# The last two groups' output projection as one stripe of 16 rows in three pieces

## The chip, the cores and the metric

The kernel runs on one core of one Trainium2 chip. The metric is the device time of one execution in microseconds (us); lower is better. A run's time is a little longer than the span that its profile shows, which goes from the first to the last instruction.

## The reference

Two independent problems, A and B, of the same shape: one decoding step of attention over a sliding window, followed by the output projection. Batch 2, one query token, D = 576, 32 query heads over 16 key/value heads of 128, cache length 16384, of which the last W = 4096 keys count; bf16.

```python
q = (x @ wq).reshape(B, Sq, Hq, Dh)            # heads first
k = repeat(k_cache[:, :, Sk - W:, :], 2)       # the last 4096 keys
v = repeat(v_cache[:, :, Sk - W:, :], 2)
p = softmax((q @ k.T) * Dh ** -0.5)
out = (p @ v).reshape(B, Sq, Hq * Dh) @ wo     # wo is 4096 x 576
...
return concatenate([a, b], axis=-1)            # 2 x 1 x 1152
```

## The kernel before

The work is cut into groups of four key/value heads: 4 groups per problem, 8 in all (NG = 8; groups 0 to 3 are A, 4 to 7 are B). A group has one K slab and one V slab per batch, 4 MB each, so 16 K slabs and 16 V slabs (NSLAB = 16). Slab i belongs to group i // 2 and batch i % 2. The slabs pass through `ring`, a buffer of four slots.

All large transfers are issued by SyncE (SP) in one order, the list `stream`: K slabs, V slabs three steps behind (LAG = 3), and now and then a piece of wo. `issue` writes one entry with the operations that it waits for, and `ensure` issues entries up to the one needed. SP waits in order: what stands behind a waiting transfer waits too.

Per group: VectorE (DVE) turns K (`make_X`), TensorE (PE) makes scores (`make_S`), the maximum goes over PE, DVE and GpSimd (POOL) (`make_max`, `make_Tm_pe`, `make_nM`, `make_bias`), ScalarE (ACT) takes exponentials, DVE turns them (`make_pT`), and PE multiplies with V (`make_PV`, 128 matmuls of 512 columns for a slab, four at a time into the bank `OTB`). `make_evac` scales the result into `tmp` and sums it into `oR`. `make_dg` spreads `oR` over partitions with one matmul into the bank TB, by a 0/1 matrix, and `make_pick` takes from that the value that each partition needs: a product with a mask on DVE (A) and a reduction. Then PE multiplies with rows of wo held in `wob` (16 rows of 576 columns on each of 128 partitions).

The projection of groups 0 to 5 goes by pairs: two groups are one stripe of wo, 16 rows in one transfer of 2304 KB ("M"), the first group on partitions 0 to 63 of `oM` and the second on 64 to 127 (`make_projm`). The last two groups, 6 and 7, are handled one by one: each has 8 rows ("W", 1152 KB), all 128 partitions belong to the one group, and the picked values lie in `oP`, spread by the matrix `selx` and picked by the mask `cm16` (`make_proj`). Group 6's 8 rows are one transfer; group 7's are three, cut by

```python
w_cuts = [0, 4, 7, 8]
```

The last row's weights are loaded ahead of its data, and its four matmuls come in two operations, one for each half of the columns that DVE and ACT evict at the end (`make_E`). For problem B each row is four matmuls of 144 columns (`cells`: two column halves at two places of the array). The last V slab arrives in two pieces, cut at key 80 of 128. `filler` puts matmuls on PE whose result nobody reads.

The end of the program is written out by hand. After the last K slab, in the order in which PE gets it: V slab 13, rows 0 to 7 of stripe 2 (groups 4 and 5), the spreading of group 6, rows 8 to 11, the sums of group 7, V slab 14, rows 12 to 15, fillers, V slab 15's first piece, spreading and pick of group 7's batch 0, fillers, V slab 15's second piece, fillers, spreading and pick of batch 1, the W rows of group 6, the W rows of group 7, the evictions and the output.

Of the kernel before, what the change touches and what calls it, by code (L numbers as in the profile page):

```python
# [63 lines left out]
def build_kernel(nc, probs, out):  # L64
# [29 lines left out]
    with es:  # L94
# [21 lines left out]
        cm16 = sb("cm16", [128, 16], FP32)  # L116
        jmask_f = sb("jmask_f", [128, 8], FP32)
        m8 = sb("m8", [128, 16, 8], FP32)
        selx = sb("selx", [128, 8, 16], FP32)
# [13 lines left out]
        oP = sb("oP", [128, 2, 8, Bb], BF16)  # L133
        oM = sb("oM", [128, 16, Bb], BF16)
# [25 lines left out]
        v_cuts = [0, 80, KJ]  # L160
        lastv_sem = [sem("lastv")]
        w_cuts = [0, 4, 7, 8]
# [54 lines left out]
        def mask(dst, view, axes, tag):  # L217
            return dve(lambda e: e.tensor_reduce(dst, view, axes, ALU.add), [p_ident_f], tag)
# [21 lines left out]
        d_cm = mask(cm16[:, 0:16], ident_f[:].rearrange("p (x q) -> p q x", q=16), AX.X, "cm16")  # L240
# [6 lines left out]
        p_sx = pool(lambda e: e.tensor_copy(selx[:], jmask_f[:, 0:8].unsqueeze(2).broadcast_to([128, 8, 16])), [d_jf], "selx")  # L247
# [83 lines left out]
        stream.append(("W", NG - 2))  # L331
        stream.append(("W", NG - 1))
        NM = NG // 2 - 1
# [13 lines left out]
        projm_first = {}  # L347

        def issue(key):
            kind, i = key  # L350
            if kind in "MW":
                n = 16 if kind == "M" else 8
                first_g = 2 * i if kind == "M" else i
                P, gl = first_g // GP, first_g % GP
                at = 0 if kind == "M" else 8 * (i % 2)
                rows = probs[P][4][gl * 1024:gl * 1024 + 128 * n, :].rearrange("(p j) n -> p j n", j=n)
                deps = ([projm_op[i - 1]] if i >= 1 else []) if kind == "M" else [projm_first[NM - 1] if i == NG - 2 else projm_op[NM - 1]]
                cuts = [(0, n, wo_sem[i % 2])]
                if i == NG - 1:
                    cuts = [(w_cuts[k], w_cuts[k + 1], ([wo_sem[1]] + lastw_sem)[k]) for k in range(3)]  # L360
                stream_dma[key] = []
                for j0, j1, sm in cuts:
                    def f(e, j0=j0, j1=j1, sm=sm):
                        return e.dma_start(wob[:, at + j0:at + j1, :].rearrange("p j n -> p (j n)"),
                                           rows[:, j0:j1, :].rearrange("p j n -> p (j n)")).then_inc(sm, 16)
                    stream_dma[key].append((j0, j1, dma_op("sp", sm, 1, f, deps, "wo%d_%d" % (i, j0))))
                return
            P, g, b = i // (2 * GP), (i // 2) % GP, i % 2
            src_t = probs[P][1] if kind == "K" else probs[P][2]
            src = src_t[b, 4 * g:4 * g + 4, Sk - W:Sk, :].rearrange("k (r j) d -> r k j d", j=KJ)  # L370
            r = slot_of[key]
            prior = uses[r][:uses[r].index(key)]
            deps = [last_reader[prior[-1]]] if prior else first_deps[r]
            cuts = [(0, KJ, ring_sem[r])]
            if key == ("V", NSLAB - 1):
                cuts = [(v_cuts[k], v_cuts[k + 1], ([ring_sem[r]] + lastv_sem)[k]) for k in range(2)]
            stream_dma[key] = []
            for c0, c1, sm in cuts:
                def f(e, c0=c0, c1=c1, sm=sm):
                    return e.dma_start(ring[:, r, c0 * 128:c1 * 128],  # L380
                                       src[:, :, c0:c1, :].rearrange("r k j d -> r k (j d)")).then_inc(sm, 16)
                stream_dma[key].append((c0, c1, dma_op("sp", sm, 1, f, deps, "%s%d_%d" % (kind, i, c0))))
# [23 lines left out]
        proj_op = {}  # L406
# [166 lines left out]
        def make_dg(G, bs=(0, 1)):  # L573
            b0, nb = bs[0], len(bs)
            sl_, p_sl = (selx, p_sx) if G >= NG - 2 else (selm, p_sm)
            n, bank, op = tb_job(lambda e, bank: e.matmul(bank[:, 0:128 * nb], sl_[:].rearrange("p h c -> p (h c)"),
                                                          oR[:, b0:b0 + nb, :].rearrange("p b d -> p (b d)"), start=True, stop=True),
                                 "dg%d_%d" % (G, b0), [ch[(G, "red%d" % b)] for b in bs] + [p_sl])
            ch[(G, "dg")] = op
            dg_job[(G, bs)] = (n, bank)  # L580

        def make_pick(G, bs=(0, 1)):
# [3 lines left out]
            tv = tmp[:, 0:128 * nb]  # L586
            if G < NG - 2:
                h0 = 64 * v
                tv = tmp[h0:h0 + 64, 0:256]
                a = dve(lambda e: e.tensor_tensor(  # L590
                    tv.rearrange("p (b c j) -> p b c j", b=2, c=8), bank[h0:h0 + 64, 0:256].rearrange("p (b c j) -> p b c j", b=2, c=8),
                    jmask_f[h0:h0 + 64, 0:8].unsqueeze(1).unsqueeze(3).broadcast_to([64, 2, 8, 16]), ALU.mult),
                    [ch[(G, "dg")], d_jf, ch["tmp"]], "A%d" % G)
                dst, q = oM[h0:h0 + 64, :, :].rearrange("p j b -> p b j"), G // 2
                free, c = [projm_op[q - 1]] if q >= 1 else [], 8
            else:
                a = dve(lambda e: e.tensor_tensor(
                    tv.rearrange("p (b c j) -> p b c j", b=nb, c=16), bank[:, 0:128 * nb].rearrange("p (b c j) -> p b c j", b=nb, c=16),
                    cm16[:, 0:16].unsqueeze(1).unsqueeze(3).broadcast_to([128, nb, 16, 8]), ALU.mult), [ch[(G, "dg")], d_cm, ch["tmp"]], "A%d" % G)
                dst = oP[:, v, :, b0:b0 + nb].rearrange("p j b -> p b j")  # L600
                free, c = [], 16
            tb_consumer[n] = a

            def f_pick(e):
                with nc.allow_low_precision(reason="one term of the c is not zero"):
                    return e.tensor_reduce(dst, tv.rearrange("p (b c j) -> p b j c", b=nb, c=c), AX.X, ALU.add)
# [14 lines left out]

        def make_projm(q, j0=0, j1=16):
            P, start = 2 * q // GP, (2 * q) % GP == 0 and j0 == 0
            ensure(("M", q))
# [13 lines left out]
            deps = [ch[(2 * q, "oP", 0)], ch[(2 * q + 1, "oP", 0)], stream_dma[("M", q)][0][2]]  # L638
            if start:
                deps += [e_ops[(P - 1, 0)], e_ops[(P - 1, 1)]] if P >= 1 else [q_ev[2]]  # L640
            projm_op[q] = pe(f, deps, "projm%d_%d" % (q, j0))
            if j0 == 0:
                projm_first[q] = projm_op[q]

        def make_proj(G):
            v = G % 2
            ensure(("W", G))
            oPs = [ch[(G, "oP", b)] for b in range(2) if (G, "oP", b) in ch]
            for j0, j1, dma in stream_dma[("W", G)]:
                held = G == NG - 1 and j1 == 8  # L650
                if held:
                    def f_w(e):
                        for h in range(2):
                            last = e.add_instruction(mybir.InstLdweights(
                                name=nc.get_next_instruction_name(), engine=mybir.EngineType.PE,
                                ins=[e.lower_ap(oP[:, v, 7, :], for_matmul_weights=True)], outs=[],
                                tile_size=(128, 32), tile_position=(0, 32 * h)))
                        return last
                    pe(f_w, oPs, "projw%d" % G)

                    for c in range(2):
                        def f_c(e, c=c):
                            for h in range(2):
                                last = cell(e, oP[:, v, 7, :], 8 * v + 7, c, h, False, True)
                            return last
                        last_cell[c] = pe(f_c, oPs + [dma], "proj%d_7%d" % (G, c))
                    continue

                def f(e, j0=j0, j1=j1):
                    for j in range(j0, j1):  # L670
                        last = cells(e, oP[:, v, j, :], 8 * v + j, False)
                    return last
                proj_op[G] = pe(f, oPs + [dma], "proj%d_%d" % (G, j0))

        def make_E(P):
# [7 lines left out]
            for h in range(2):  # L683
                def f_first(e, h=h):
                    return e.dma_start(out[:, 0, h * NH:(h + 1) * NH], out_sb[:, h * NH:(h + 1) * NH]).then_inc(out_sem, 16)
                dma_op(("sp", "act")[h], out_sem, 1, f_first, [e_ops[(0, 0)], e_ops[(0, 1)], stream_dma[("W", NG - 1)][1][2]], "out0_%d" % h)
# [61 lines left out]
        make_projm(NM - 1, 0, 8)  # L748
        make_dg(NG - 2)
        make_projm(NM - 1, 8, 12)  # L750
# [5 lines left out]
        make_projm(NM - 1, 12, 16)  # L756
        filler(4)
        make_evac(i + 2)
        make_PV(i + 3, (0,))
        make_dg(NG - 1, (0,))  # L760
        make_pick(NG - 1, (0,))
        filler(4)
        make_PV(i + 3, (1,))
# [4 lines left out]
        make_proj(NG - 2)  # L768
        make_proj(NG - 1)
# [93 lines left out]
```

## Time and profile before

| | before |
|---|---|
| median of 3 runs | 363.09 us (362.92 to 363.18) |
| profiled execution | 363.1 us |
| its span | 361.8 us |
| mean granted TensorE clock | 0.887 |
| busy PE / DVE / ACT / POOL | 63% / 60% / 13% / 7% |
| traffic | 153.28 MB, mean 424 GB/s |
| wo of B, last two groups: issue to landing | 1152 KB 19.4 us; 576 KB 10.2; 432 KB 10.9; 144 KB 10.8 |

How to read it: the span is what the profile covers; 1.3 us of the profiled execution lie outside. A busy share is an average over the whole span, and an engine can be idle for most of it and still set the end. A transfer's time to landing holds its time in the queue: all transfers share 16 DMA engines, which work through them in the order of issue, each on its part of every transfer. In a timeline row the columns are the start, the duration, engine, line, operation, output and inputs, count, and in brackets the idle time before it with what ended that. A line of a view by windows has, for each engine, the busy time and the number of instructions, then the granted clock (1.00 is full speed), the share of the DMA engines and GB/s.

### The profile page before, as it was taken

Reading aid. Unit: us, or ns where it says so; the run is one execution under the profiler, and the core shown is the slowest. Engines: PE = TensorE matmul, PEld = TensorE weight load, DVE = VectorE, ACT = ScalarE, POOL = GpSimd, SP = SyncE. Lnnn points to the kernel's source line nnn. Section 1 sums busy time; section 2 is a strip of 40 time slices with the busy share of each in tenths; the row PEclk is TensorE's granted clock in tenths of the full one; section 3 lists DMA queues with packets and bytes.
Section 4 is the critical chain, followed back from the end, with each engine's and each line's share of the span. In section 5 each row is a group of like instructions: output and inputs, shape, how many; then the busy total and the mean of one; then the engine's idle time right before and its main releaser. Section 6 shows DMA issues by size and latency. Waiting matters only on the chain.

```text
span 361.8 us, 2701 instructions
## 1 busy us (share of the span) xinstructions
PE 229.0 (63%) x1357; PEld 56.1 (16%) x943; DVE 218.6 (60%) x150; ACT 45.4 (13%) x77; POOL 24.3 (7%) x84
## 2 busy tenths in 40 slices
PE   0397687767464866671696656662776675667575
PEld 0010111112110211120121211110112121112222
DVE  0811898495949392924919493952927776675522
ACT  1002100040031002200005000500005000500500
POOL 4200101100010001000010000000010000001000
PEclk9999698969999889888798998899589897869989
DMA  8999999999999999999999999999999999999996
GB/s 327 449 428 420 442 426 424 446 413 446 417 447 420 442 422 422 439 438 420 438 424 434 431 438 412 448 420 442 424 435 429 428 438 420 434 442 420 427 417 258
DMA packets 6088, 153.28 MB, mean 424 GB/s; under 512 B 684, under 2 KB 828, under 8 KB 1084
## 3 DMA queue, kind: packets, MB, share of 16 engines
q1 hardware_dynamic: 6056, 153.10, 98.7%
q8 instruction: 9, 0.15, 0.2%
q14 instruction: 3, 0.02, 0.0%
q10 hardware_dynamic: 20, 0.01, 0.0%
HBM read 153.10 MB, written 0.00 MB: 423 GB/s over the span
## 4 chain that ended last, share of the span: by engine, by line
DMA 49%; DVE 24%; PE 16%; issue 8%; ACT 1%; POOL 1%; SPq 0%
DMA ring<-in_B_k_cache_dram 25%; DVE xt L436 15%; DMA ring<-in_B_v_cache_dram 9%; DMA ring<-in_B_wq_dram 7%; DMA ring<-in_A_k_cache_dram 6%; PE st L266 6%; PE st L462 5%; DMA wob<-in_B_wo_dram 3%; DVE oR L569 2%; DVE mx L470 2%; DVE pT L509 2%; PE pj L266 2%; DVE tmp L562 2%; PE ot L539 1%; ACT pR L500 1%
## 5 line engine op out<-in xcount | busy, mean ns | idle before, releaser
L462 PE MATMUL st<-xt,zq 128*128 128x512 bf16 x256 | 119.3, 466 | 93.6 <-DVE xt L436 93.6
L436 DVE STREAM_TRANSPOSE xt<-ring 128x4096 f32<-128x4096 f32 x32 | 141.6, 4429 | 33.5 <-DMA ring<-in_A_k_cache_dram 18.2
L266 PE MATMUL st<-xt,zq 128*128 128x512 bf16 x256 | 118.0, 461 | 0.0
L500 ACT ACTIVATE pR<-st,bias 128x512 bf16<-128x512 f32 x32 | 40.0, 1419 | 219.0 <-DVE bias L493 219.0
L462 PEld LDWEIGHTS st<-xt,zq 128*128 128x128 bf16 x256 | 28.3, 110 | 211.5 <-DVE xt L436 110.0
L539 PE MATMUL ot<-ring,pT 128*32 128x512 bf16 x512 | 32.0, 393 | 8.3 <-DMA ring<-in_B_v_cache_dram 8.3
L493 DVE SCALAR_TENSOR_TENSOR bias<-vmask,tb,offm 128x4 f32<-128x4 f32 x8 | 1.8, 224 | 37.1 <-PE tb L490 37.1
L523 DVE TENSOR_REDUCE ssum<-tb 128x2 f32<-128x8 f32 x8 | 1.3, 162 | 33.4 <-PE tb L520 33.4
L428 POOL TENSOR_TENSOR zq<-qs,bmask 128x64 bf16<-128x64 bf16 x32 | 8.6, 292 | 161.2 <-PE st L266 140.3
L509 DVE STREAM_TRANSPOSE pT<-pR 128x2048 bf16<-128x2048 bf16 x8 | 18.4, 2303 | 0.7 <-ACT pR L500 0.7
L562 DVE SCALAR_TENSOR_TENSOR tmp<-ot,rsb,dmask 128x512 f32<-128x512 f32 x16 | 11.5, 719 | 9.4 <-PE ot L539 9.4
L281 PE MATMUL ot<-ring,pT 128*32 128x512 bf16 x18 | 7.6, 421 | 15.1 <-DMA ring<-in_A_wq_dram 14.5
L539 PEld LDWEIGHTS ot<-ring,pT 128*32 128x32 bf16 x512 | 12.4, 99 | 23.7 <-DMA ring<-in_B_v_cache_dram 10.5
L569 DVE TENSOR_REDUCE oR<-tmp 128x128 f32<-128x512 f32 x15 | 15.6, 1039 | 0.5
L266 PE MATMUL pj<-ring,pT 128*32 128x512 bf16 x36 | 12.1, 422 | 0.0
L266 PE MATMUL pj<-wob,oM 128*2 128x288 bf16 (+1 forms) x64 | 10.2, 256 | 0.0
L470 DVE TENSOR_REDUCE mx<-st 128x2 f32<-128x1024 f32 x8 | 9.7, 1208 | 0.1
L500 ACT ACTIVATION_READ_ACCUMULATOR pR<-st,bias 128x1 f32 x32 | 9.1, 283 | 0.0
L636 PE MATMUL pj<-wob,oM 128*2 128x288 bf16 x32 | 7.9, 286 | 0.0
L224 DVE TENSOR_TENSOR xt<-xt,hmask 4x1152 bf16<-4x1152 bf16 x2 | 2.8, 1398 | 8.4 <-DMA xt<-in_A_x_dram 8.4
L266 PE MATMUL st<-ring,pT 128*32 128x512 bf16 x18 | 7.4, 414 | 0.0
L472 POOL TENSOR_TENSOR mv<-mx,v 128x2 f32<-128x2 f32 x8 | 1.6, 195 | 80.0 <-DVE mx L470 80.0
(71 smaller groups left out, 79.5 us busy)
## 6 DMA issues: line engine op xcount, KB each, us to landing
ring<-in_A_k_cache_dram SPq DMA_DIRECT2D x8, 4096.0 KB, 24.9
ring<-in_A_v_cache_dram SPq DMA_DIRECT2D x8, 4096.0 KB, 30.0
ring<-in_B_k_cache_dram SPq DMA_DIRECT2D x8, 4096.0 KB, 28.5
ring<-in_B_v_cache_dram SPq DMA_DIRECT2D x7, 4096.0 KB, 31.8
ring<-in_A_wq_dram SPq DMA_DIRECT2D x1, 4608.0 KB, 13.6
ring<-in_B_wq_dram SPq DMA_DIRECT2D x1, 4608.0 KB, 24.1
wob<-in_A_wo_dram SPq DMA_DIRECT2D x2, 2304.0 KB, 29.8
ring<-in_B_v_cache_dram SPq DMA_DIRECT2D x1, 2560.0 KB, 26.9
```

What stands on the lines that cost most here:

```text
L266: return e.add_instruction(mybir.InstMatmult(name=nc.get_next_instruction_name(), engine=mybir.EngineType.PE, ins=[e.lower_ap(mv_), e.lowe ...
L281: last = e.matmul(QB[c], wt, mv_, start=first, stop=True, skip_group_check=True)
L428: last = e.tensor_tensor(dst, src, msk, ALU.mult)
L436: Xop[(t, jh)] = dve(lambda e: e.transpose(xt[:, jh, :].bitcast(FP32).rearrange("p (kp x kt) -> p x kp kt", kp=2, kt=2), ring[:, r, jh * H ...
L462: last = e.matmul(ob, wt, mv_, start=first, stop=True, skip_group_check=True)
L470: ch[(G, "max")] = dve(lambda e: e.tensor_reduce(mx[:], st[:, :].rearrange("p (x t) -> p t x", t=2), AX.X, ALU.max), [Sop[(2 * G + 1, 1)]] ...
L500: last = e.activation(pR[:].rearrange("p (x k) -> p k x", k=4)[:, kv, :], st[:, :].rearrange("p (x t) -> p t x", t=2)[:, kv % 2, :], ACTF.Exp,
L509: pT_op[G] = dve(lambda e: e.transpose(pT[:, v, :].rearrange("p (w j q) -> p j w q", w=4, q=8), pR[:].rearrange("p (j w q) -> p j w q", w= ...
L539: last = e.matmul(OTB[32 * c:32 * c + 32, :], pT[:, v, base + 32 * c:base + 32 * c + 32], ring[:, r, jj * 128:(jj + 4) * 128], start=rd == ...
L562: evac_op[i] = dve(lambda e: e.scalar_tensor_tensor(tv, o, rsb[:, v, b:b + 1], dm, ALU.mult, ALU.mult), deps, "ev%d" % i)
L569: ch[(G, "red%d" % b)] = dve(lambda e: e.tensor_reduce(oR[:, b, :], tmp[:].rearrange("p (j d) -> p d j", j=4), AX.X, ALU.add), [evac_op[i] ...
L636: last = e.matmul(PJ[0], oM[:, j, :], mv_, start=start and j == 0, stop=True, skip_group_check=True)
```

## The change

The last two groups are handled like the others: their part of wo is a fourth stripe (NM = 4), 16 rows with group 6 on the lower 64 partitions and group 7 on the upper. It comes in three transfers of 12, 3 and 1 rows. Each waits only for the rows of the stripe before that it overwrites (`projm_rows`). `oM` exists twice, `oP`, `selx` and `cm16` are gone. The last V slab is cut at key 96 instead of 80, spreading and pick of group 7's batch 0 stand ahead of that slab's first piece, and the filler behind stripe 2 has three matmuls instead of four.

```diff
-        v_cuts = [0, 80, KJ]
+        v_cuts = [0, 96, KJ]
-        w_cuts = [0, 4, 7, 8]
+        m_cuts = [0, 12, 15, 16]
...
-        d_cm = mask(cm16[:, 0:16], ident_f[:].rearrange("p (x q) -> p q x", q=16), AX.X, "cm16")
-        p_sx = pool(lambda e: e.tensor_copy(selx[:], jmask_f[:, 0:8].unsqueeze(2).broadcast_to([128, 8, 16])), [d_jf], "selx")
...
-        stream.append(("W", NG - 2))
-        stream.append(("W", NG - 1))
-        NM = NG // 2 - 1
+        NM = NG // 2
+        stream.append(("M", NM - 1))
...
+            if kind == "M":
+                P, gl = 2 * i // GP, 2 * i % GP
+                rows = probs[P][4][gl * 1024:gl * 1024 + 2048, :].rearrange("(p j) n -> p j n", j=16)
+                cuts = [(0, 16, wo_sem[i % 2])]
+                if i == NM - 1:
+                    cuts = [(m_cuts[k], m_cuts[k + 1], ([wo_sem[1]] + lastw_sem)[k]) for k in range(3)]
...
+                    deps = [projm_rows[i - 1][j1]] if i >= 1 else []
...
         def make_projm(q, j0=0, j1=16):
...
             deps = [ch[(2 * q, "oP", 0)], ch[(2 * q + 1, "oP", 0)], stream_dma[("M", q)][0][2]]
+            if q == NM - 1:
+                deps = oPs_last() + [dma for c0, c1, dma in stream_dma[("M", q)] if c0 <= j0 and j1 <= c1]
...
-        make_projm(NM - 1, 0, 8)
+        make_projm(NM - 2, 0, 8)
         make_dg(NG - 2)
-        make_projm(NM - 1, 8, 12)
+        make_projm(NM - 2, 8, 12)
         make_pick(NG - 2)
...
-        make_projm(NM - 1, 12, 16)
-        filler(4)
+        make_projm(NM - 2, 12, 16)
+        filler(3)
         make_evac(i + 2)
-        make_PV(i + 3, (0,))
         make_dg(NG - 1, (0,))
         make_pick(NG - 1, (0,))
         filler(4)
+        make_PV(i + 3, (0,))
         make_PV(i + 3, (1,))
         make_evac(i + 3)
         filler(3)
         make_dg(NG - 1, (1,))
         make_pick(NG - 1, (1,))
-        make_proj(NG - 2)
-        make_proj(NG - 1)
+        make_projm(NM - 1, 0, 12)
+        make_projm(NM - 1, 12, 15)
+        make_last_row()
         make_E(NPROB - 1)
```

`oPs_last` lists the picks of groups 6 and 7 in both batches; `make_last_row` loads the weights of row 15 ahead and runs its four matmuls in two operations, as the last row of group 7 did.

More of the change, by code (lines that the diff above doesn't have):

```diff
@@ L115, in build_kernel @@
         dmask = sb("dmask", [128, 4], FP32)
-        cm16 = sb("cm16", [128, 16], FP32)
         jmask_f = sb("jmask_f", [128, 8], FP32)
         m8 = sb("m8", [128, 16, 8], FP32)
-        selx = sb("selx", [128, 8, 16], FP32)
         selm = sb("selm", [128, 16, 8], FP32)
@@ L132, in build_kernel @@
         rsb = sb("rsb", [128, 2, 2], FP32)
-        oP = sb("oP", [128, 2, 8, Bb], BF16)
-        oM = sb("oM", [128, 16, Bb], BF16)
+        oM2 = [sb("oM%d" % k, [128, 16, Bb], BF16) for k in range(2)]
         out_sb = sb("out_sb", [Bb, NOUT], BF16)
@@ L346, in build_kernel @@
         projm_op = {}
-        projm_first = {}
+        projm_rows = {}
         def issue(key):
             kind, i = key
[L351 to L360, printed above, removed]
+            if kind == "M":
[4 more added lines that the diff above has]
+                    cuts = [(m_cuts[k], m_cuts[k + 1], ([wo_sem[1]] + lastw_sem)[k]) for k in range(3)]
                 stream_dma[key] = []
@@ L363, in f @@
                     def f(e, j0=j0, j1=j1, sm=sm):
-                        return e.dma_start(wob[:, at + j0:at + j1, :].rearrange("p j n -> p (j n)"),
+                        return e.dma_start(wob[:, j0:j1, :].rearrange("p j n -> p (j n)"),
                                            rows[:, j0:j1, :].rearrange("p j n -> p (j n)")).then_inc(sm, 16)
+                    deps = [projm_rows[i - 1][j1]] if i >= 1 else []
                     stream_dma[key].append((j0, j1, dma_op("sp", sm, 1, f, deps, "wo%d_%d" % (i, j0))))
@@ L405, in build_kernel @@
         evac_op = {}
-        proj_op = {}
         last_cell = {}
@@ L574, in make_dg @@
             b0, nb = bs[0], len(bs)
-            sl_, p_sl = (selx, p_sx) if G >= NG - 2 else (selm, p_sm)
-            n, bank, op = tb_job(lambda e, bank: e.matmul(bank[:, 0:128 * nb], sl_[:].rearrange("p h c -> p (h c)"),
+            n, bank, op = tb_job(lambda e, bank: e.matmul(bank[:, 0:128 * nb], selm[:].rearrange("p h c -> p (h c)"),
                                                           oR[:, b0:b0 + nb, :].rearrange("p b d -> p (b d)"), start=True, stop=True),
-                                 "dg%d_%d" % (G, b0), [ch[(G, "red%d" % b)] for b in bs] + [p_sl])
+                                 "dg%d_%d" % (G, b0), [ch[(G, "red%d" % b)] for b in bs] + [p_sm])
             ch[(G, "dg")] = op
@@ L585, in make_pick @@
             n, bank = dg_job[(G, bs)]
[L586 to L601, printed above, removed]
+            h0, q = 64 * v, G // 2
+            tv = tmp[h0:h0 + 64, 0:128 * nb]
+            a = dve(lambda e: e.tensor_tensor(
+                tv.rearrange("p (b c j) -> p b c j", b=nb, c=8), bank[h0:h0 + 64, 0:128 * nb].rearrange("p (b c j) -> p b c j", b=nb, c=8),
+                jmask_f[h0:h0 + 64, 0:8].unsqueeze(1).unsqueeze(3).broadcast_to([64, nb, 8, 16]), ALU.mult),
+                [ch[(G, "dg")], d_jf, ch["tmp"]], "A%d_%d" % (G, b0))
+            dst = oM2[q % 2][h0:h0 + 64, :, b0:b0 + nb].rearrange("p j b -> p b j")
+            free = [projm_rows[q - 2][16]] if q >= 2 else []
             tb_consumer[n] = a
@@ L605, in f_pick @@
                 with nc.allow_low_precision(reason="one term of the c is not zero"):
-                    return e.tensor_reduce(dst, tv.rearrange("p (b c j) -> p b j c", b=nb, c=c), AX.X, ALU.add)
+                    return e.tensor_reduce(dst, tv.rearrange("p (b c j) -> p b j c", b=nb, c=8), AX.X, ALU.add)
             ch[(G, "oP", b0)] = dve(f_pick, [a] + free, "oP%d_%d" % (G, b0))
@@ L620, in cells, with oPs_last @@
             return last
+        def oPs_last():
+            return [ch[(G, "oP", b)] for G in (NG - 2, NG - 1) for b in range(2) if (G, "oP", b) in ch]
         def make_projm(q, j0=0, j1=16):
             P, start = 2 * q // GP, (2 * q) % GP == 0 and j0 == 0
+            oM = oM2[q % 2]
             ensure(("M", q))
@@ L641, in make_projm @@
             projm_op[q] = pe(f, deps, "projm%d_%d" % (q, j0))
[L642 to L671, printed above, removed]
@@ new lines, in make_projm, with make_last_row, f_w, f_c @@
+            for k in range(j0 + 1, j1 + 1):
+                projm_rows.setdefault(q, {})[k] = projm_op[q]
+        def make_last_row():
+            q = NM - 1
+            oM = oM2[q % 2]
+            def f_w(e):
+                for h in range(2):
+                    last = e.add_instruction(mybir.InstLdweights(
+                        name=nc.get_next_instruction_name(), engine=mybir.EngineType.PE,
+                        ins=[e.lower_ap(oM[:, 15, :], for_matmul_weights=True)], outs=[],
+                        tile_size=(128, 32), tile_position=(0, 32 * h)))
+                return last
+            pe(f_w, oPs_last(), "projw")
+            for c in range(2):
+                def f_c(e, c=c):
+                    for h in range(2):
+                        last = cell(e, oM[:, 15, :], 15, c, h, False, True)
@@ L672, in f @@
                     return last
-                proj_op[G] = pe(f, oPs + [dma], "proj%d_%d" % (G, j0))
+                last_cell[c] = pe(f_c, oPs_last() + [stream_dma[("M", q)][2][2]], "proj15_%d" % c)
         def make_E(P):
@@ L685, in f_first @@
                     return e.dma_start(out[:, 0, h * NH:(h + 1) * NH], out_sb[:, h * NH:(h + 1) * NH]).then_inc(out_sem, 16)
-                dma_op(("sp", "act")[h], out_sem, 1, f_first, [e_ops[(0, 0)], e_ops[(0, 1)], stream_dma[("W", NG - 1)][1][2]], "out0_%d" % h)
+                dma_op(("sp", "act")[h], out_sem, 1, f_first, [e_ops[(0, 0)], e_ops[(0, 1)], stream_dma[("M", NM - 1)][1][2]], "out0_%d" % h)
             evs = [dve(lambda e: e.tensor_copy(out_w[:, 0:NQ], PJW[0]), [last_cell[0]], "E%d_0" % P),
```

## The prediction

> **What bounds the kernel now.** I read the page's slices first. In its second part the 16 DMA engines are busy in every slice but the last, and the traffic only falls in the last 9 us:
>
> ```profile
> DMA  8999999999999999999999999999999999999996
> GB/s 327 449 428 420 442 426 424 446 413 446 417 447 420 442 422 422 439 438 420 438 424 434 431 438 412 448 420 442 424 435 429 428 438 420 434 442 420 427 417 258
> ```
>
> So 153 MB are streamed without a hole, and an edit in the middle of the run moves nothing. What an edit of the tail is worth lies between the last landings and the end. Next the DMA view (KB of each issue, us from issue to landing) for wo of B:
>
> ```profile
> wob<-in_B_wo_dram SPq DMA_DIRECT2D x1, 1152.0 KB, 19.4
> wob<-in_B_wo_dram SPq DMA_DIRECT2D x1, 576.0 KB, 10.2
> wob<-in_B_wo_dram SPq DMA_DIRECT2D x1, 432.0 KB, 10.9
> wob<-in_B_wo_dram SPq DMA_DIRECT2D x1, 144.0 KB, 10.8
> ```
>
> Issued at 337.54 and (three in a row) from 348.13, they land at 356.9, 358.3, 359.4 and 359.8. Then the timeline of the tail (start, us, engine, line; 16 weight loads are 8 rows of wo, two loads and four matmuls to a row):
>
> ```profile
> 354.20 0.83 PE L539 MATMUL ot<-ring,pT 128*32 128x512 bf16 x12 [1.14 <-DMA ring<-in_B_v_cache_dram]
> 357.10 0.90 PEld L614 LDWEIGHTS pj<-wob,oP 128*2 128x2 bf16 x16
> 357.53 0.39 DVE L606 TENSOR_REDUCE oP<-tmp 128x8 bf16<-128x128 f32 x1
> 358.47 0.43 PEld L614 LDWEIGHTS pj<-wob,oP 128*2 128x2 bf16 x8 [0.47 <-issue]
> 359.45 0.28 PEld L614 LDWEIGHTS pj<-wob,oP 128*2 128x2 bf16 x6 [0.55 <-DMA wob<-in_B_wo_dram]
> 360.10 0.30 DVE L687 CAST out_w<-pj 34x144 bf16<-34x144 f32 x1 [2.18 <-PE pj L266]
> ```
>
> Group 6's eight rows run at 357.10, ahead of and beside group 7's last pick (it ends at 357.92); four more at 358.47 when their piece lands; three at 359.45 when theirs lands; the eighth right behind, the evictions at 360.10. The chain of waits agrees: before 360.15 it is "DMA wob" up to 359.41 and then the last four rows. So PE follows each landing within 0.1 us and has no backlog.
>
> **The change, part by part.** The profiled execution took 363.1 us with a span of 361.8, so 1.3 us lie around it; the median of the runs is 363.09, the same. The sum is made against 363.1.
>
> Rows 0 to 11: now eight rows need only group 6 and 1152 KB. In the stripe every row holds both groups in its 128 contraction partitions (16 rows of 1152 B to a partition, group 6 on the lower 64), so no row can start before group 7's last pick nor before the first piece, which is 12 rows, 1728 KB. That is 1152 + 576: its last byte is where the 576 KB piece ends today. The work stays 16 rows, 64 matmuls. A row costs 0.125 us (in the timeline its pairs of matmuls start at 357.10, 357.16, 357.22, 357.28). So 12 rows from 358.50, the first matmul behind that landing today, end at 358.50 + 12 x 0.125 = 360.00. The three rows that start at 359.45 today then start at 360.00; their piece has landed by 359.41. From there all is as today: four rows, eviction, output. Term: 360.00 - 359.45 = **+0.55 us**, all on the path. The seam between row operations I take at nothing: today the eighth row follows the seventh without a hole.
>
> Packets: one DMA less, so 128 packets less. In the trace's packet records one of 9216 B takes 351 ns, one of 4608 B 180 ns and one of 20480 B 765 ns, so 0.0368 ns per byte, and one of 13824 B about 520 ns against 531 for the two. Eight on each engine: 0.09 us, with the dropped completion write 0.1. Bounds: 0 (the 9216 B stretch ran no slower than the 12288 B stretch: 1152 KB in 2.8 us, 1536 KB in 3.7 us) to 0.1; I take **-0.10**, as the records are direct.
>
> V cut at 96: the last piece leaves 8 matmuls for 12, one round of four, 0.22 us; the pick would end at 357.70 instead of 357.92. Cover: the 1728 KB landing at 358.3; were that 0.6 us earlier, the 0.22 would count. The first piece carries 512 KB more, 1.2 us at 425 GB/s, lands at 351.7, and its 24 matmuls (6 x 0.22 + 0.2) end at 353.2, ahead of 354.16. Nothing.
>
> Pick of batch 0 moved ahead: its expansion matmul waits on PE for the reduction that ends at 349.47. Queued behind that wait are four fillers and V's first piece; expansion 0.49 and fillers 0.86 end near 350.9, before 351.7. Nothing. One filler less (0.22): nothing by itself, see the rival.
>
> SP queue: the first wo piece waits for rows 0 to 11 of the stripe before (PE at 339.75) instead of 0 to 7 (337.5). Behind it on SP stand only the other two pieces and the outputs, which wait till 348.13 anyway; V fills the engines till 354.16, so 2.2 us of 16 us are used. Nothing, bounded by zero both sides as long as V is queued. Two issues instead of three after 348.13: also covered.
>
> Masks: cm16 (0.36 us on DVE) and selx (1.42 us on POOL) fall away near 15 us, where the second projection waits for its weights till 25.40. Picks on 64 partitions cost what those on 128 cost (64x256: 0.43 and 0.59; 128x256: 0.43 and 0.61). oM doubled: frees earlier. Nothing.
>
> Sum: 363.10 + 0.55 - 0.10 = **363.55**.
>
> **The rivals.** *Half clock in the last rows (slower).* The clock's records change on a grid of 3.41 us. Windows on that grid (us, then PE busy; the three figures at the end are clock, DMA share, GB/s):
>
> ```profile
> 145.67:149.08 3.41, 1.42 (x6) 0.38 (x4) 3.38 (x3) 1.54 (x4) 0.20 (x1) 1.00 1.11 474
> 149.08:152.50 3.42, 3.42 (x10) 0.58 (x4) 3.42 (x3) 0.00 (x0) 0.00 (x0) 0.50 0.96 412
> 200.28:203.70 3.42, 1.51 (x7) 0.38 (x4) 1.85 (x1) 0.00 (x0) 0.00 (x0) 1.00 1.02 441
> 203.70:207.11 3.41, 3.15 (x15) 1.06 (x8) 0.42 (x3) 0.00 (x0) 0.54 (x2) 1.00 0.94 404
> 319.75:323.16 3.41, 1.08 (x5) 0.10 (x1) 3.41 (x1) 0.00 (x0) 0.00 (x0) 1.00 1.03 442
> 323.16:326.58 3.42, 2.96 (x7) 0.54 (x4) 0.40 (x1) 0.00 (x0) 0.00 (x0) 0.50 0.96 412
> 354.99:358.40 3.41, 2.38 (x41) 1.04 (x19) 2.15 (x5) 0.00 (x0) 0.00 (x0) 1.00 0.90 364
> ```
>
> A window with PE busy 1.42 or less is followed by clock 0.50, one with 1.51 by 1.00; 1.5 us decides. Today any 3.41 us before the end hold over 2.2, since group 6's rows fill 357.1 to 358.1. Changed, the 3.41 us before 358.40 hold V and fillers up to 355.56 (0.57) and the expansion (0.49): 1.06. If a grid line falls between about 358.0 and 359.4, the rest of the rows runs at half clock, where matmuls take twice as long (rounds of V every 0.43 us at 344.81 and 345.24, clock 0.50, against 0.22 from 350.51, five rounds in 1.26 us with 0.38 for the last). Price: the row time left, 2.0 us for a line at 358.4, 1.1 at 359.4, some 1.6 on average: 363.55 + 1.6 = 365.15. For it: 1.06 is clearly under 1.42. Against it: in this profile the lines stand at 353.88, 357.30 and 360.71, and the window to 357.30 would hold 1.36 + 0.49 = 1.85, enough. Which place the line takes in other executions this one trace can't show; of 3.41 us, 1.4 are harmful, 0.41.
>
> [...]
>
> *The backlog doesn't form.* If the 12 rows' piece lands by 357.8, PE starts behind the pick and ends 2.0 us later, and with 0.2 us to the eviction at 360.0 against 360.10: 363.0. Against it: the 576 KB piece lands at 358.3 today and the bytes ahead of it are the same.
>
> *A later landing.* The large piece is whole only with its slowest engine's last packet; were that engine one packet of 13824 B further back, 0.52 us, the end would be 364.05. *A gain over 0.2%* would need the whole stream 0.7 us shorter; only the 0.1 us of packets speaks for it: 362.3.
>
> **How the numbers follow.** Forecast 0.49, backlog absent 0.07: both within 0.2% (0.73 us, about what a measurement of this kernel can tell from no change), so 0.56. Half clock 0.35 (0.41 less some doubt), later landing 0.04: slower 0.39. Faster 0.05. The likeliest case has 363.2 to 363.8. The range runs from 362.9 to 365.4: it leaves out the gain (0.05) and the grid lines before 358.55 (four tenths of that rival, 0.14).
>
> **What would show it.** In the changed profile: no wo rows before 358.3; 24 weight loads in one run of 1.5 us from about 358.4; no wait for a DMA at row 12; evictions near 360.55; landings of the three pieces within 0.15 us of 358.3, 359.4 and 359.8; V's first piece near 351.7; clock 1.00 to the end, or 0.50 with row pairs 0.12 us apart. The prediction is wrong if rows run before 358, if PE waits for the 432 KB piece, or if the stream ends over 0.3 us off.

## The result and the profile after

The changed kernel takes 364.5 us in the median of 16 executions (363.37 to 365.45), the kernel before 363.09. The ratio of the means is 1.0036, 95% interval 1.0027 to 1.0046: slower, by 0.4%. One of the 16 executions of the kernel before took 760.99 us and is left out of the ratio; the other fifteen lie at 362.92 to 363.20. The median hides that the executions fall into two groups: seven at 363.37 to 363.88 (median 363.60) and nine at 364.41 to 365.45 (median 365.05), with nothing between 363.88 and 364.41. The nine are called the late ones below. The kernel before has no second group: of 33 executions beside the last experiments all lie at 362.87 to 363.68.

The profiled execution took 363.37 us, span 362.1, so it is one of the first group. No late execution of this kernel was profiled, and the mean clock of the span doesn't tell the groups apart (0.863 to 0.882 in the first, 0.855 to 0.878 in the second). The page's traffic rows look like those of before: the DMA engines are busy in every slice but the last, which has 238 GB/s for 258. The DMA view of it:

```profile
ring<-in_B_v_cache_dram SPq DMA_DIRECT2D x1, 1024.0 KB, 29.9
wob<-in_B_wo_dram SPq DMA_DIRECT2D x1, 1728.0 KB, 18.4
wob<-in_B_wo_dram SPq DMA_DIRECT2D x1, 432.0 KB, 11.3
wob<-in_B_wo_dram SPq DMA_DIRECT2D x1, 144.0 KB, 11.2
```

And the timeline of its tail:

```profile
354.05 0.61 PE L529 MATMUL ot<-ring,pT 128*32 128x512 bf16 x8 [1.00 <-DMA ring<-in_B_v_cache_dram]
357.17 0.36 DVE L587 TENSOR_REDUCE oM<-tmp 64x16 bf16<-64x128 f32 x1
358.26 1.80 PEld L595 LDWEIGHTS pj<-wob,oM 128*2 128x2 bf16 x30 [1.66 <-DVE oM L587]
358.29 0.23 PE L595 MATMUL pj<-wob,oM 128*2 128x144 bf16 x2 [1.49 <-DMA wob<-in_B_wo_dram]
360.44 0.30 DVE L664 CAST out_w<-pj 34x144 bf16<-34x144 f32 x1 [2.91 <-PE pj L261]
```

The last pick ends at 357.53, 0.4 us sooner than before, and nobody profits: PE stands idle for 1.49 us until the 1728 KB piece lands (358.16), then loads weights for 15 rows in one go. No wait for the 432 KB piece is left; PE is behind it. From the last V piece to the eviction it takes 360.44 - 354.05 = 6.39 us, against 360.10 - 354.20 = 5.90 before: the backlog is 0.49 us. This is the first group. Windows of the same execution (us, PE busy; clock, DMA share and GB/s at the end), the first two on its clock grid:

```profile
353.77:357.18 3.41, 1.86 (x13) 0.51 (x11) 1.78 (x5) 0.00 (x0) 0.00 (x0) 1.00 0.98 411
357.18:360.59 3.41, 2.17 (x64) 1.41 (x32) 0.50 (x2) 0.10 (x1) 0.00 (x0) 1.00 0.34 128
354.99:358.40 3.41, 1.02 (x8) 0.44 (x6) 1.86 (x5) 0.00 (x0) 0.00 (x0) 1.00 0.87 357
```

Here the grid falls kindly: a line at 357.18, behind a window with 1.86 us of work. The third row is the window that a line at 358.40 would close: 1.02 us of work where the kernel before had 2.38.

### The profile page after: what moved, and what is told of

The parts are those of the page before. It is cut to its first block, busy times and chain, and to the rows that moved or that the text cites. A ratio compares the mean times of both kernels' runs of the same rounds, so it can differ in the third digit from the quotient of the medians.

```text
span 362.1 us, 2695 instructions
## 1 busy us (share of the span) xinstructions
PE 230.9 (64%) x1355; PEld 56.6 (16%) x943; DVE 218.1 (60%) x149; ACT 45.5 (13%) x77; POOL 24.1 (7%) x83
## 4 chain that ended last, share of the span: by engine, by line
DMA 43%; DVE 28%; PE 18%; issue 8%; ACT 1%; POOL 1%; SPq 0%
DMA ring<-in_B_k_cache_dram 17%; DVE xt L426 17%; DMA ring<-in_B_v_cache_dram 8%; DMA ring<-in_B_wq_dram 7%; DMA ring<-in_A_k_cache_dram 6%; PE st L261 6%; PE st L452 6%; DMA wob<-in_B_wo_dram 5%; DVE oR L559 3%; PE pj L261 3%; DVE pT L499 2%; DVE tmp L552 2%; DVE mx L460 2%; ACT pR L490 1%; PE pj L621 1%
## 5 line engine op out<-in xcount | busy, mean ns | idle before, releaser
L452 PE MATMUL st<-xt,zq 128*128 128x512 bf16 x256 | 121.0, 472 | 91.2 <-DVE xt L426 91.2
L261 PE MATMUL st<-xt,zq 128*128 128x512 bf16 x256 | 119.7, 468 | 0.0
L261 PE MATMUL pj<-wob,oM 128*2 128x144 bf16 (+1 forms) x98 | 12.3, 245 | 0.0
L565 PE MATMUL tb<-oR,selm 128*128 128x256 f32 (+1 forms) x18 | 5.9, 408 | 4.1 <-DVE oR L559 1.6
```

Of the source, the lines that this page charges most:

```text
L261: return e.add_instruction(mybir.InstMatmult(name=nc.get_next_instruction_name(), engine=mybir.EngineType.PE, ins=[e.lower_ap(mv_), e.lowe ...
L452: last = e.matmul(ob, wt, mv_, start=first, stop=True, skip_group_check=True)
```

## The experiments

Each was timed in five rounds beside the kernel before (median 363.07 to 363.09 there), the first four on one chip and the other four on another. "PE work in a window" is PE's busy time in 3.41 us.

**Fillers in the hole ahead of the rows.**

```diff
 (the changed kernel)
         make_pick(NG - 1, (1,))
+        filler(5)
         make_projm(NM - 1, 0, 12)
```

> The changed kernel with five more filler matmuls (1.1 us) between the last expansion and the first row of the stripe, where PE waits for wo. Theory (the changed kernel's spread is TensorE's clock: a window of 3.41 us with under some 1.5 us of PE work ends just before or in the last rows): no window is that empty any more, so all runs lie at 363.3 to 363.7, with clock 1.00 to the end; what is left against 363.09 is the backlog of rows. Rival (the spread comes from the wo pieces landing later in some executions): more PE work changes nothing, about half the runs stay above 364.3.

Measured: 363.59 us, ratio 1.0021 (1.0012 to 1.0030); six of nine executions at 363.38 to 363.66, three at 364.54 to 364.74. So with matmuls whose result nobody reads the median is 0.9 us lower, which speaks against the landings; nine executions in two groups are few, and the next experiment and the one with both holes filled decide it. The expectation that no late execution is left failed. The next windows were read for that: first the one ahead of 356.6, then the one ahead of 358.4.

```profile
353.17:356.58 3.41, 1.54 (x16) 0.27 (x10) 1.47 (x3) 0.00 (x0) 0.00 (x0) 1.00 1.01 426
354.99:358.40 3.41, 2.22 (x10) 0.32 (x3) 2.08 (x5) 0.00 (x0) 0.00 (x0) 1.00 0.83 343
```

The hole ahead of the rows is closed (2.22), but a second window is thin: around the last V piece, 1.54. Whether it accounts for three of nine is open. In this profile a grid line closes a window of under 1.6 us there at only some 0.3 us of the 3.41 us of places, and of the windows with 1.5 to 1.6 us in the profiles of before and after two of eight were followed by 0.50 (last section).

**No fillers behind the last V piece.**

```diff
 (the changed kernel)
         make_evac(i + 3)
-        filler(3)
         make_dg(NG - 1, (1,))
```

> The changed kernel without the three fillers behind the last V piece, which nobody waits for. Clock theory: every place of the window's grid now has a window with under 1.5 us of PE work before the rows, so nearly all runs are slow: 364.8 to 365.5, median about 365.3, and the profile has clock 0.50 in the rows with pairs of matmuls about 0.12 us apart, at the same landing (358.3). Rival (landings): as the changed kernel, median about 364.5 with half the runs under 364, rows 0.0625 us apart at any time.

Measured: 365.40 us (365.18 to 365.53, all five executions), ratio 1.0063 (1.0050 to 1.0076). The profile shows the half clock itself. Timeline, then the windows on this execution's grid:

```profile
354.25 0.62 PE L529 MATMUL ot<-ring,pT 128*32 128x512 bf16 x8 [1.01 <-DMA ring<-in_B_v_cache_dram]
356.51 0.49 PE L565 MATMUL tb<-oR,selm 128*128 128x128 f32 x2 [1.65 <-DVE oR L555]
358.47 3.36 PEld L595 LDWEIGHTS pj<-wob,oM 128*2 128x2 bf16 x30 [1.66 <-DVE oM L587]
358.50 0.28 PE L595 MATMUL pj<-wob,oM 128*2 128x144 bf16 x2 [1.50 <-DMA wob<-in_B_wo_dram]
359.05 0.33 PE L261 MATMUL pj<-wob,oM 128*2 128x144 bf16 x2
359.17 0.33 PE L595 MATMUL pj<-wob,oM 128*2 128x144 bf16 x2
362.23 0.30 DVE L664 CAST out_w<-pj 34x144 bf16<-34x144 f32 x1 [4.49 <-PE pj L261]
```

```profile
355.00:358.41 3.41, 0.49 (x2) 0.30 (x2) 2.05 (x5) 0.00 (x0) 0.00 (x0) 1.00 0.84 346
358.42:361.83 3.41, 3.33 (x58) 1.93 (x30) 0.00 (x0) 0.00 (x0) 0.00 (x0) 0.50 0.11 39
```

The piece is in use at 358.47, as before the change; the same 30 weight loads take 3.36 us instead of 1.80: a window with 0.49 us of PE work closed at 358.41, and the next runs at clock 0.50, pairs of matmuls 0.12 us apart instead of 0.06. From the V piece to the eviction it takes 362.23 - 354.25 = 7.98 us, 1.59 more than in the changed kernel's profile. So three matmuls whose result nobody reads, left out, cost that much.

**The stripe in four pieces.**

```diff
 (the changed kernel)
-        m_cuts = [0, 12, 15, 16]
+        m_cuts = [0, 8, 12, 15, 16]
...
-        make_projm(NM - 1, 0, 12)
+        make_projm(NM - 1, 0, 8)
+        make_projm(NM - 1, 8, 12)
```

> The changed kernel with the stripe in four pieces of 8, 4, 3 and 1 rows, so the first eight rows need 1152 KB as before the change. Theory (backlog of rows behind a 12-row piece, and the idle hole ahead of it): the eight rows run from about 357.6, behind the last pick, four from 358.5, three from 359.4: evictions near 360.1, time 363.0 to 363.2, no slow group of runs. Rival (the stripe itself costs: both groups in one row, picks on 64 partitions, or its deeper waits): 363.4 or more.

Measured: 363.15 us, ratio 1.0008 (0.9998 to 1.0018); nine of eleven executions at 362.95 to 363.50, two at 364.59 and 364.73. Its timeline:

```profile
354.23 0.61 PE L529 MATMUL ot<-ring,pT 128*32 128x512 bf16 x8 [1.00 <-DMA ring<-in_B_v_cache_dram]
357.76 1.40 PEld L595 LDWEIGHTS pj<-wob,oM 128*2 128x2 bf16 x24 [0.98 <-DVE oM L587]
359.50 0.28 PEld L595 LDWEIGHTS pj<-wob,oM 128*2 128x2 bf16 x6 [0.34 <-DMA wob<-in_B_wo_dram]
360.14 0.30 DVE L664 CAST out_w<-pj 34x144 bf16<-34x144 f32 x1 [2.44 <-PE pj L261]
```

Twelve rows start behind the pick (357.76), PE is again ahead of the 432 KB piece (it waits 0.34 us), and the eviction is back at 5.91 us behind the V piece. The stripe itself, with both groups in a row and picks on 64 partitions, costs nothing that these runs can tell; its 12-row first piece does. The two late executions were not expected.

**The wait alone, without the stripe.**

```diff
 (the kernel before, make_proj)
+            if G == NG - 2:
+                ensure(("W", NG - 1))
+                oPs = oPs + [ch[(NG - 1, "oP", b)] for b in range(2)] + [stream_dma[("W", NG - 1)][0][2]]
```

> The kernel before, with one wait added: group 6's rows wait for group 7's picks and for the 576 KB piece, as the stripe's rows do; layout, transfers and picks are those of before. Theory: this wait alone makes the backlog and the hole, so the fast runs lie at 363.5 to 363.8 and about four in ten runs or more at 364.4 to 365.5. Rival (the stripe's own layout or transfers cost the time): 363.1 as before, in all runs.

Measured: 363.50 us, ratio 1.0020 (1.0010 to 1.0030); eight of twelve at 363.39 to 363.58, two at 363.79 and 363.87, two at 365.11 and 365.20. Its tail, and the window that a line at 358.40 would close:

```profile
354.28 0.83 PE L539 MATMUL ot<-ring,pT 128*32 128x512 bf16 x12 [1.15 <-DMA ring<-in_B_v_cache_dram]
358.49 1.80 PEld L614 LDWEIGHTS pj<-wob,oP 128*2 128x2 bf16 x30 [1.44 <-DVE oP L606]
360.66 0.30 DVE L690 CAST out_w<-pj 34x144 bf16<-34x144 f32 x1 [2.67 <-PE pj L266]
```

```profile
354.99:358.40 3.41, 1.36 (x9) 0.39 (x3) 2.14 (x5) 0.00 (x0) 0.00 (x0) 1.00 0.90 365
```

The backlog is there in full, eviction at 360.66 behind a V piece at 354.28, 6.38 us, with the layout and transfers of before. The late executions, two of twelve, are fewer than the four in ten expected and than the changed kernel's nine of sixteen. This kernel has V cut at 80, and its window ahead of 358.40 holds 1.36 us of PE work, not 1.02; that this is the reason was not tested.

**The rest alone, without the stripe.** V cut at 96, the pick ahead, one filler less, in the kernel before.

> The kernel before with only the rest of the change: V cut at 96, pick of batch 0 ahead of V's first piece, one filler less; group 6 and 7 keep their own rows and transfers. Theory (the stripe's 12-row wait makes both the backlog and the hole; the rest only takes 0.2 us of PE work out ahead of 356.6, where a window is at 1.5 to 1.6 us of work): most runs at 363.0 to 363.2, at most two in ten at 363.5 to 364.7. Rival (the rest of the change makes the slow group): about half the runs above 364.3.

Measured: 363.15 us, ratio 1.0004 (0.9995 to 1.0013); nine of eleven at 362.91 to 363.29, two at 363.71 and 363.77, none above. As long as group 6's rows fill the hole, the rest costs nothing clear of the noise; the two lie just above the highest of 33 executions of the kernel before, 363.68. That the rest adds to the late executions of the stripe is not excluded by this.

**Both holes filled.** The first experiment's kernel, with `filler(5)` for `filler(3)` behind the last V piece; and the four-piece stripe with the same edit.

> The changed kernel with both holes filled: five fillers instead of three behind the last V piece and five ahead of the stripe's rows. Clock theory with two holes: no slow run is left, all at 363.3 to 363.7, which is the backlog alone. Rival (a part of the slow runs has another cause): three in ten stay at 364.5 to 364.8, as with the second hole open.

> The stripe in four pieces (8, 4, 3, 1) and five fillers instead of three behind the last V piece, so that the window ending near 356.6 holds some 1.9 us of PE work instead of 1.5. Theory (the few slow runs of the four-piece kernel come from a grid line near 356.6): all runs at 363.0 to 363.3. Rival (they come from the hole before the rows or from the transfers): two in ten stay at 364.6.

Measured: the 12-row stripe 363.51 us (363.28 to 363.58, all eleven), ratio 1.0011 (1.0002 to 1.0020); the four-piece stripe 363.04 us (362.86 to 363.38, all eleven), ratio 0.9999 (0.9990 to 1.0008). The window around the last V piece in the one and the other:

```profile
352.95:356.36 3.41, 1.95 (x15) 0.36 (x11) 1.47 (x3) 0.00 (x0) 0.00 (x0) 1.00 1.02 432
353.14:356.55 3.41, 1.94 (x18) 0.27 (x10) 1.47 (x3) 0.00 (x0) 0.00 (x0) 1.00 1.00 414
```

From 1.54 to 1.95, and the late executions are gone, in the first kernel by this edit alone. None of eleven against the changed kernel's nine of sixteen leaves little to chance; against the three of nine with one hole filled it is few. (In the four-piece kernel the edit also lifts the window ahead of the rows, so there it doesn't say which of the two was thin.) What is left of the changed kernel's loss, 363.51 - 363.07 = 0.44 us, is the backlog: from the V piece to the eviction the first kernel takes 360.35 - 353.96 = 6.39 us, as the changed kernel did. The four-piece stripe is as fast as the kernel before, not faster: in both the three rows behind the 432 KB piece wait for its landing, 0.34 us up to 359.51 here and 0.55 us up to 359.45 there.

**V cut at 80 in the filled kernel.** The first experiment's kernel with `v_cuts = [0, 80, KJ]`.

> The changed kernel with five fillers ahead of the stripe's rows (as in the first run) and the last V slab cut at key 80 again, so that four more V matmuls (0.2 us) run behind its last piece. If the V cut is what brought the window near 356.6 under the 1.5 us: no slow run, all at 363.3 to 363.7. If not: three in ten at 364.5 to 364.8 as with the cut at 96.

Measured: 363.52 us, ratio 1.0015 (1.0006 to 1.0024); eight of eleven at 363.39 to 363.62, three at 363.90 to 364.04, none at 364.5. The four V matmuls lift that window only from 1.54 to 1.58. So the V cut may have a part in the late executions; three of nine against none of eleven, with a lift of 0.04 us, doesn't show it, and the three at 364 stay unexplained.

## Why the prediction was right, and where it was off

The range held, and the mechanism of both groups was named; the time given for the likeliest case, 363.55, is that of the smaller group (363.60). The median, 364.50, is just inside the late group, which the prediction held to be the less likely case (0.39 against 0.56 for no change); the range held because it took in most of that rival too.

Rows 0 to 11 (+0.55): confirmed. Behind the V piece the tail grew by 0.49 us; adding the wait alone to the kernel before gave the same 6.38 us; with the clock held up the whole kernel is 0.44 us over the one before.

Packets (-0.10): not seen. From the V piece to the first row's weights the changed kernel took 358.26 - 354.05 = 4.21 us, and the kernel with the wait alone, whose 1152 and 576 KB go separately, 358.49 - 354.28 = 4.21. The lower bound, nothing, was the better choice. That the sum, +0.45, still agrees with the 0.44 to 0.49 measured is luck: a backlog taken 0.06 us too large and a gain of 0.10 that wasn't there nearly cancel.

V cut, one filler less, pick ahead: "Nothing" held for the path and failed for the clock. The 0.22 us of V matmuls was counted as hidden work that may go. It also was a part of the 1.58 us of PE work in the window ahead of 356.5, where the same profile has 0.50 behind windows of 1.42 and 1.57 us, and the cover that the prediction named, the landing, doesn't cover that. So its sentence that any 3.41 us before the end hold over 2.2 is wrong for a line near 356.5.

The rival's price: right for the group, too high for one place. Forecast 365.15, the second group's median 365.05. For a line at 358.4 the prediction had 2.0 us, all row time left; the kernel without fillers had its line at 358.41 and lost 1.59. Half clock lasted one window there, from 358.42 to 361.83, and the last six matmuls took 0.35 us, as they did in the changed kernel's profile at clock 1.00.

The rival's chance: the step that failed. It was worked out as 0.41 of the grid's places, from one hole, taken down to 0.35 "less some doubt", and used as the chance that the whole measurement is slow. But the place is not the same in every profile: relative to the first instruction a grid line lay at 357.30 in that of before, at 357.18 in that of after, at 358.41 in the one without fillers. These are three kernels with one execution each; if the place also differs between the executions of one kernel, as the two groups suggest, a share of the places is a share of the executions and forecasts a mixture: with 0.41 of them late the mean would be 363.55 + 0.41 x 1.6 = 364.2, already 0.3% over 363.1. (The measured mean is 364.39.) Nine of sixteen were late, 0.56; by chance alone, 0.41 gives as many about once in six times. The second hole was put at nothing, and its share is not settled: with the first closed, three of nine executions were late, and none of eleven with both closed. The figure behind it, "1.5 us decides", was read from a choice of windows. The profile of before also has this pair, in which half clock follows 1.57 us:

```profile
261.72:265.14 3.42, 1.57 (x8) 0.32 (x4) 2.76 (x2) 0.00 (x0) 0.00 (x0) 1.00 0.98 422
265.14:268.55 3.41, 3.41 (x10) 0.58 (x5) 0.00 (x0) 0.00 (x0) 0.00 (x0) 0.50 1.00 432
```

With it, the window of 1.58 us ahead of 356.5 would have been in doubt before any V matmul was taken from it. As the likeliest case was chosen by this chance, the forecast of no change fell with it.

## What to carry to other kernels

Joining transfers joins waits: a piece is worth only what the work behind its last byte can start with. Here, with both holes filled, twelve rows behind one landing of 1728 KB cost 0.44 us (363.51 against 363.07), and the same rows behind landings of 1152 and 576 KB nothing (363.04). So the work of a tail should be cut at the landings, not at round sizes. An idle TensorE was not free of charge in these runs: three matmuls whose result nobody reads, left out, cost 1.59 us at the end. Before work is taken from it or moved into one burst near the end, add up its busy time in every 3.41 us ahead of the burst, at any place of the grid, and look up in the kernel's own profiles which windows were followed by half clock; in those of before and after none with 1.6 us or more was, of 104 at full clock. And when a kernel's times fall into two groups, look for a state that differs between the executions, and force it both ways, as the fillers did here.

## What the runs showed of the hardware

In the profiles of before and after, every clock record but the last lasts a whole multiple of 3.41 us. The table has PE's busy time in each window of that grid, and the clock of the window behind it; the windows ahead of a profile's first clock record, 19.4 and 19.3 us, are left out.

| PE busy in the window | its clock | windows | followed by 1.00 | followed by 0.50 |
|---|---|---|---|---|
| 1.60 to 3.41 us | 1.00 | 104 | 104 | 0 |
| 1.50 to 1.57 us | 1.00 | 8 | 6 | 2 |
| 0 to 1.44 us | 1.00 | 36 | 0 | 36 |
| 2.65 to 3.41 us | 0.50 | 38 | 38 | 0 |
| 0 to 2.43 us | 0.50 | 12 | 0 | 12 |

The same count with the profiles of the first four experiments, six in all: at full clock, every window from 1.6 us on was followed by full clock; from 1.5 to 1.6, two of 16 were followed by 0.50; from 1.3 to 1.5, 30 of 35; from 0.8 to 1.3, all 45. At 0.50, none of the 19 windows with 1.6 to 2.6 us was followed by full clock, and every one over 2.6 was (the kernel with both holes filled has one of 2.61 that was not).

So in these runs a window with some 2 us of PE work kept full clock where it was granted (2.01 us at 347.06 before, then 1.00), and didn't bring it back where it wasn't (1.84 us at 302.68 before, then 0.50 again; 2.43 us at 254.90, the same). The kernel without fillers dropped to 0.50 with no idle stretch of PE over 1.65 us in the window ahead. The busy times are the profile's, with modelled ends, so that windows within some 0.01 us of a bound can fall on either side.
